# An input transposed by the loading DMA instead of TensorE, its first transform in 64-row tile pairs, and a rebuilt start order

## The chip, the core and the metric

The kernel runs on one core of a Trainium2 chip. The metric is the device time of one execution in microseconds. A core has five engines that run side by side, each through its own list of instructions in order: TensorE for matmuls (PE; its weight loads are shown apart as PEld), VectorE (DVE), ScalarE (ACT), GpSimd (POOL) and SyncE (SP). Engines wait for each other through semaphores. DMA transfers are issued from the queues of SP, ACT and POOL and all share 16 DMA engines. [...]

## What is computed

One input x (2048 rows of 640, bf16) goes through two branches, mixed row by row with a gate g.

```python
g = _sigmoid((x * gate_w).sum(-1, keepdims=True))
a = _A_ref(x, A_wqkv, A_wo)
b = _B_ref(x, B_A_re, B_A_im, B_B_re, B_B_im, B_C_re, B_C_im, B_log_dt, B_Dskip)
return g * a + (1 - g) * b
```

Branch A is attention with 32 heads of 20: q, k and v are projections of x, every position looks at 8 positions with distance 2, and the result is projected with wo. Branch B is a state-space convolution: for each of the 640 channels a filter K of 2048 taps is built from 192 complex modes (a sum of exponentials), and x is convolved with it through Fourier transforms of length 4096; x * Dskip is added.

## The kernel before

Everything is cut into tasks, 1,274 in the list `main` and 304 in `tail`. A task is added with `pl.add(name, engines, duration, function, ...)`. The order in which tasks are issued is not found at build time: `ORDER` is a table of numbers, one for each task, that gives the next task's index as a step from the last, with a letter where ACT or DVE may do it (A or D). `emit` walks the table and ties each engine's instructions together in that order.

The stages that the change and the prediction touch are these.

- **Loads of x and weights** (`Attn.loads`). `xl` holds four loads of x, 512 rows each; `wl` holds three loads of the projection weights (q, k, v) into the buffer `bufA`. They are issued on SP, between the parameter loads of `SSMParams.build` (`cre`, `bre`, `cim`, `bim`, `aim`, `are`, and the small `ldt`).
- **Turning x** (`Attn.window`). x arrives with positions on the partitions (tile `xn`). The projections need the 640 features on the partitions, so ten tasks `turn` multiply 128x128 blocks with an identity on PE, eight to a task, into the PSUM ring `ar`, and ten evictions `tev` put the result into `xT`, a part of `bufA`. The ring `ar` has two buffers (pool `pa`) and also serves the filter generator and the first transforms.
- **Projections** (`plan_late`, line 311, 300 matmuls of 512 columns, tile `tb`), evicted to `qA`, `kA`, `prj`, `pv` or `vst`. Each of the 60 evictions may be done by ACT or DVE.
- **The gate** (`plan_gate`, line 219): 80 narrow matmuls over all of `xT`.
- **Filter parameters** (`SSMParams.build`): a chain of operations on [128, 960] tiles over DVE and ACT, with logarithm, exponential and arctangent. Its ten results `pc` (a ring of four) are stored by SP to the DRAM tensor `Sprm` and read back as the tile `L`, by SP and, for one half of the first `L`, by POOL.
- **Filter generator** (`KGen.plan`): ten rounds. PE makes arguments from `L` (line 801), ACT takes sines (line 816) and exponentials (line 818) of them, DVE multiplies these (`pt`, `qq`), PE sums (line 856, `kps`), and ACT or DVE evicts to `E`.
- **Attention core** (`plan_core`): products on DVE (`prod`, line 375; `pv`, line 449), sums on PE, and the gated output `ga` (lines 489 and 491), all mixed with the generator's rounds.
- **First transforms** (`first`, line 1300): `f1` and `fk` for the filter, `fu` for the input (tile `Usb`). One `fu` task multiplies four 128x128 pieces with the 128x256 matrix `F1c`, which is block diagonal: rows of group g only meet columns of group g. `F1c` is block diagonal in four groups of 32 rows and 64 columns.
- **Tail** (`fft_conv`): the second transform (`fp`, line 1073), products of spectra, the inverse transforms (lines 1134 and 1164), the mix with the gate and the output. Its four PSUM buffers of `fp` are opened when all PSUM pools of `main` are closed.

## Time and profile before

| what | value |
|---|---|
| time of the runs, median (lowest, highest) of 3 | 336.16 us (335.34, 339.4) |
| span of the profiled execution | 335.4 us |
| granted TensorE clock, mean | 0.980 |
| DMA mean rate | 136 GB/s |
| x loads on SP | 4 of 640 KB |
| weight loads on SP | 3 of 800 KB |
| parameter loads on SP and ACT | 6 of 240 KB |
| turning matmuls on PE | 80, 264 ns each |
| first transform of the input on PE | 80, 275 ns each |

The profile comes from one execution. Its span (from the first to the last instruction) is 335.4 us; no time of that execution is given apart from its span, which stands 0.06 us above the fastest run and 0.8 below the median. Busy time of an engine is the time in which one of its instructions runs; matmuls overlap, so the mean of a matmul's length is longer than the time it adds. In rows of the timeline the first number is the start, the second the length; the bracket tells how long the engine had been idle and what ended that. In the page's second part the span is cut into 40 slices of 8.4 us, and a digit is the busy share in tenths.

### The profile page before, as it was taken

The numbers are of one execution on the slowest core, as the hardware profiler recorded it, in microseconds if no ns is written. First come the engines' busy times: TensorE is split into PE (matmuls) and PEld (weight loads), VectorE is DVE, ScalarE is ACT, GpSimd is POOL, SyncE is SP. The second block draws the span as 40 slices with busy tenths as digits, with TensorE's granted clock in tenths as the row PEclk, the third lists the DMA queues.
The fourth block names the chain that finished last, engine by engine and source line by source line (L and its number), as shares of the span: only waits on it lengthen the run. The fifth ranks groups of instructions, "written<-read, shape, count | busy, mean of one in ns | idle before, by whom it ended". The sixth has DMA issues, their size and how long they took to land. (4 is left out here: it accounts for less than half of the span.)

```text
span 335.4 us, 11982 instructions
## 1 busy us (share of the span) xinstructions
PE 285.5 (85%) x5181; PEld 171.0 (51%) x5214; DVE 294.2 (88%) x401; ACT 293.4 (87%) x433; POOL 62.3 (19%) x94
## 2 busy tenths in 40 slices
PE   0367999997899999999998799999999899996850
PEld 0334563444445555445554344556677676665740
DVE  1997988798989999999999979999686799999881
ACT  1789736999899999999999799999987889998990
POOL 8700043020005000101412341211040000000062
PEclk9999999999999999999999989999999999999985
DMA  8984435437107110524874887365565527666056
GB/s 253 356 264 113 119 91 159 86 91 170 26 9 153 27 24 8 149 62 141 199 190 119 186 208 161 93 118 124 154 207 221 180 64 216 159 123 100 4 136 182
DMA packets 45975, 45.68 MB, mean 136 GB/s; under 512 B 25098, under 2 KB 39738, under 8 KB 45922
## 3 DMA queue, kind: packets, MB, share of 16 engines
q1 hardware_dynamic: 39928, 27.90, 30.3%
q0 software_dynamic: 5248, 16.39, 20.2%
q8 instruction: 41, 0.67, 0.9%
q10 hardware_dynamic: 746, 0.61, 0.6%
q14 instruction: 12, 0.10, 0.1%
HBM read 30.88 MB, written 14.01 MB: 134 GB/s over the span
## 5 line engine op out<-in xcount | busy, mean ns | idle before, releaser
L311 PE MATMUL tb<-bufA 128*128 128x512 bf16 x267 | 73.5, 391 | 4.2 <-issue 1.4
L816 ACT ACTIVATE big<-ar 128x740 bf16<-128x740 int16 (+1 forms) x72 | 56.7, 858 | 1.4 <-PE ar L801 1.2
L818 ACT ACTIVATE big<-ar 128x848 bf16<-128x848 f32 x60 | 50.1, 905 | 0.2
L801 PE MATMUL ar<-Rarg,L 64*128 64x212 bf16 (+4 forms) x600 | 46.5, 253 | 3.5 <-ACT big L816 1.9
L449 DVE TENSOR_TENSOR pv<-vc,asb 128x2048 bf16<-128x2048 bf16 x40 | 48.2, 1217 | 0.3 <-PE tb L456 0.3
L311 PEld LDWEIGHTS <-bufA 128*128 128x128 bf16 x300 | 31.2, 122 | 28.5 <-issue 12.3
L856 PEld LDWEIGHTS <-pt 128*32 128x32 bf16 (+1 forms) x2560 | 25.3, 92 | 35.7 <-issue 33.2
L856 PE MATMUL kps<-qq,pt 128*32 128x21 bf16 (+1 forms) x2560 | 36.6, 173 | 6.0 <-issue 5.1
L838 DVE TENSOR_TENSOR pt<-big 128x1024 bf16<-128x1024 bf16 x48 | 32.8, 701 | 4.3 <-ACT big L816 2.2
L801 PEld LDWEIGHTS <-L 64*128 64x128 bf16 x600 | 20.8, 94 | 25.2 <-issue 22.4
L480 PE MATMUL tb<-wo_sb,oT 128*128 128x320 bf16 x160 | 29.9, 306 | 0.2
L507 ACT ACTIVATE sp_u<-fp 128x640 bf16<-128x640 f32 x31 | 23.9, 953 | 0.8 <-PE fp L1073 0.8
L375 DVE TENSOR_TENSOR prod<-prj 128x2048 bf16<-128x2048 bf16 x20 | 24.0, 1218 | 0.2 <-PE lg L381 0.2
L375 DVE TENSOR_TENSOR prod<-qA,kA 128x2048 bf16<-128x2048 bf16 x20 | 23.9, 1217 | 0.2 <-PE lg L381 0.2
L507 ACT ACTIVATE sp_k<-fp 128x640 bf16<-128x640 f32 x29 | 22.6, 969 | 1.1 <-PE fp L1073 1.1
L456 PE MATMUL tb<-pv,ind 128*64 128x512 bf16 (+1 forms) x192 | 23.2, 353 | 0.0
L368 POOL DMA_DIRECT2D vc<-vS x16 | 11.5, 723 | 59.0 <-DVE pv L449 55.0
L840 DVE TENSOR_TENSOR qq<-big 128x1344 bf16<-128x1344 bf16 x24 | 21.2, 883 | 0.0
L1191 POOL DMA_DIRECT2D out_dram<-ot x14 | 7.7, 558 | 72.3 <-DVE ot L1173 72.3
L1073 PEld LDWEIGHTS <-PHI 128*128 128x128 bf16 x160 | 15.5, 97 | 8.1 <-issue 1.1
L489 ACT ACTIVATE ga<-tb,g_sb 128x320 bf16<-128x320 f32 x29 | 15.6, 550 | 3.4 <-PE tb L480 3.1
L480 PEld LDWEIGHTS <-oT 128*128 128x128 bf16 x160 | 13.1, 98 | 7.1 <-issue 3.1
(171 smaller groups left out, 547.9 us busy)
## 6 DMA issues: line engine op xcount, KB each, us to landing
vc<-vS POOLq DMA_DIRECT2D x16, 327.5 KB, 6.4
xn<-in_A_x_dram SPq DMA_DIRECT2D x4, 640.0 KB
gaS<-ga SPq DMA_DIRECT2D x8, 320.0 KB
Usb<-in_A_x_dram POOLq DMA_DIRECT2D x8, 320.0 KB, 5.7
gaF<-gaS SPq DMA_DIRECT2D x8, 320.0 KB
bufA<-in_A_wqkv_dram SPq DMA_DIRECT2D x3, 800.0 KB
Sprm<-pc SPq DMA_DIRECT2D x10, 240.0 KB
L<-Sprm SPq DMA_DIRECT2D x76, 30.0 KB
```

Of the source, the lines that this page charges most:

```text
L311: nc.tensor.matmul(ppf, self.wq[:, which, kt, e::5], self.xT[:, c0 // 1024, kt, c0 % 1024:c0 % 1024 + SC], start=(kt == 0), stop=(kt == NK ...
L375: nc.vector.tensor_tensor(b[e][:], q[:, e, o:o + C].unsqueeze(1).to_broadcast([128, W, C]), win(k[:, e, :], o, W, DIL, C), ALU.mult)
L449: nc.vector.tensor_tensor(o, vw, b["asb"][:].unsqueeze(2).to_broadcast(sh), ALU.mult)
L456: nc.tensor.matmul(b["op", e][64 * a:64 * a + 64, 0:n, :], ind[:, 32:96], b["pv", e][:, w, a, 0:n, :], start=(w == 0), stop=(w == 3), skip ...
L480: nc.tensor.matmul(apf[:, :320], b["oT"][:, e, i * 128:(i + 1) * 128], wo_sb[:, e, hf * 320:(hf + 1) * 320], start=(e == 0), stop=(e == 4))
L507: nc.scalar.activation(o, i, ACT.Identity)
L801: nc.tensor.matmul(ar[:, g2, a0:a0 + ncol], L[rows, sb, gv, l0:l0 + 128], R[rows, c0:c0 + ncol], start=True, stop=True, tile_position=(64 ...
L816: nc.scalar.activation(d_[:, :, s0 * QW:s1 * QW], ar[:].bitcast(I16)[:, :, 0:2 * (s1 - s0) * QW:2], ACT.Sin, scale=SCL)
L818: nc.scalar.activation(dst[:, gp::2].rearrange("p g s n -> p g (s n)"), ar[:, :, 0:2 * EW], ACT.Exp)
L838: nc.vector.tensor_tensor(pt[:, :, k, :], gg[:, :, ::-1] if k else gg, e1, ALU.mult)
L840: nc.vector.tensor_tensor(qq[:], trg[:, :, KI:].rearrange("p a (v m) -> p a v m", v=2), exq[:, :, KI:].unsqueeze(2).to_broadcast([128, 32, ...
L856: nc.tensor.matmul(kps[32 * g:32 * g + 32, h, NM * ql:NM * ql + NM], pt[rows, k, v, :], qq[rows, k, v, :], start=(g not in started), stop= ...
```

## The change

The loads of x become DMA transposes that write `xT` directly. The tile `xn`, the ten turning tasks and their evictions are gone.

```diff
-        xr = self.x.rearrange("(i p) d -> p i d", p=128)
-        xl = [lambda sc=sc: nc.sync.dma_start(xn[:, 4 * sc:4 * sc + 4], xr[:, 4 * sc:4 * sc + 4]) for sc in range(4)]
+        xl = [lambda sc=sc: nc.sync.dma_start_transpose(self.xT[:, sc // 2, :, 512 * (sc % 2):512 * (sc % 2) + 512], self.x[512 * sc:512 * sc + 512]) for sc in range(4)]
...
-            def turn(_, hf=hf, kt=kt, b=b):
-                tx = b["tx"] = pa.tile([128, 2, 512], F32, name="ar")
-                for i in range(8):
-                    nc.tensor.matmul(tx[:, i // 4, (i % 4) * 128:(i % 4) * 128 + 128], self.xn[:, 8 * hf + i, kt * 128:(kt + 1) * 128], self.ident[:], start=True, stop=True)
-
-            def ev(en, hf=hf, kt=kt, b=b):
-                evict(nc, en, self.xT[:, hf, kt, :], b["tx"][:].rearrange("p a b -> p (a b)"))
```

The loads come in another order: log_dt first, x and weights in turn, the identity and the gate weights after the first exponential.

```diff
+        nc.scalar.dma_start(ldt[:], log_dt.rearrange("(p k) -> p k", k=5))
         load(nc.sync, "cre", C_re); load(nc.scalar, "bre", B_re)
         load(nc.sync, "cim", C_im); load(nc.scalar, "bim", B_im)
-        nc.scalar.dma_start(ldt[:], log_dt.rearrange("(p k) -> p k", k=5))
-        nc.scalar.dma_start(g5[:], gate_w.rearrange("(k p) -> k p", p=128))
-        at_.load_ident()
-        xl[0]()
         load(nc.sync, "aim", A_im)
-        xl[1]()
-        for w_ in wl:
-            w_()
+        xl[0](); wl[0](); xl[1](); wl[1]()
         load(nc.sync, "are", A_re)
-        xl[2](); xl[3]()
+        wl[2](); xl[2](); xl[3]()
...
         nc.scalar.activation(dtb[:], ldt[:], ACT.Exp)
+        nc.scalar.dma_start(g5[:], gate_w.rearrange("(k p) -> k p", p=128))
+        at_.load_ident()
```

Products with dt may now be made by ACT in five pieces, the sine table is loaded by a small operation of its own, and half of the first `L` is read by ACT's queue, not POOL's.

```diff
-            tt("tau", "tau", "aim", "dtc", ALU.mult, rdy=9.6)
+            scaled("tau", "aim", dtc, 9.6)
...
+        def scaled(o, a, m, rdy):
+            def fn(e):
+                if e == "D":
+                    V.tensor_tensor(t[o][:], t[a][:], m[:].unsqueeze(2).to_broadcast(SH), ALU.mult)
+                else:
+                    for k in range(5):
+                        SCA.activation(t[o][:, k], t[a][:, k], ACT.Identity, scale=m[:, k:k + 1])
...
+        self.warm = pl.add("wsin", "A", 0.2, lambda _: SCA.activation(sn[:], bias[0.5], ACT.Sin), after=[x for x in pl.tasks if "A" in x.dur], table="sin")
...
-                    (self.nc.gpsimd if gs == (1,) else self.nc.sync).dma_start(L[64 * g + 2:64 * g + 2 + 4 * NPC, :, v, l0:l0 + NST], src)
+                    (self.nc.scalar if gs == (1,) else self.nc.sync).dma_start(L[64 * g + 2:64 * g + 2 + 4 * NPC, :, v, l0:l0 + NST], src)
```

One `fu` task is now eight matmuls of 128 columns: rows 0 to 63 with the first half of `F1c`, rows 64 to 127 with the second. Its eviction reads the same 1024 values in another arrangement.

```diff
+                if name == "fu":
+                    by = b["by"] = b["bp"][:].rearrange("p a (b f) -> p (a b) f", f=64).rearrange("p (g q) f -> p g q f", g=4)
+                    for ql in range(4):
+                        for r in range(2):
+                            nc.tensor.matmul(by[:, 2 * r:2 * r + 2, ql], sf[64 * r:64 * r + 64, 4 * n + ql::st], P["F1c"][64 * r:64 * r + 64, 128 * r:128 * r + 128],
+                                             start=True, stop=True, skip_group_check=True, tile_position=(64 * r, 0))
+                    return
```

In the tail the first half of each `fp` pair takes its buffer from the ring `ar` of the main part, which stays open, and the second half from a new pool of two.

```diff
-                    fp = spec[nm, ro, h] = q["ps"].tile([128, 2, 512], F32, name="fp")
+                    fp = spec[nm, ro, h] = (q["ps"] if h else pa).tile([128, 2, 512], F32, name="fp", tag="fp" if h else "ar")
```

Both tables of `ORDER` are new throughout; of `main` the first numbers are shown.

```diff
 ORDER = {"main": (
-    "7 -7 15 -14 1 1166 -1164 56 -57 3 2 -3 6 1 1 39 -43 1 51A -8A -25 -14 2 38 1D 1 1A -32 33 1A -42 1 69 1 -57 72 -56 57 "
...
+    "1148 -1134 -14 52 1 2 -54 3 6 -8 1 3 1 1 3 1 -7 8 -4 18 -5 8 -15 1 7 8 -10 35 -2 3 10 1 1D 13 -3 -47D 48 -63 1 63D -47 "
```

What the new order does is shown at three places. First SP's queue at the start (`DMA` rows are loads and stores, `Sprm<-pc` the parameter results), before and then now:

```order
L583 DMA cre<-in_B_C_re_dram 128x960
L583 DMA cim<-in_B_C_im_dram 128x960
L186 DMA xn<-in_A_x_dram 128x4x640
L583 DMA aim<-in_B_A_im_dram 128x960
L186 DMA xn<-in_A_x_dram 128x4x640
L187 DMA bufA<-in_A_wqkv_dram 128x5x640 x3
L583 DMA are<-in_B_A_re_dram 128x960
L186 DMA xn<-in_A_x_dram 128x4x640 x2
L654 DMA Sprm<-pc 640x1x192 x10
```

```order
L561 DMA cre<-in_B_C_re_dram 128x960
L561 DMA cim<-in_B_C_im_dram 128x960
L561 DMA aim<-in_B_A_im_dram 128x960
L178 DMA_TRANSPOSE bufA<-in_A_x_dram 128x5x512
L179 DMA bufA<-in_A_wqkv_dram 128x5x640
L178 DMA_TRANSPOSE bufA<-in_A_x_dram 128x5x512
L179 DMA bufA<-in_A_wqkv_dram 128x5x640
L561 DMA are<-in_B_A_re_dram 128x960
L179 DMA bufA<-in_A_wqkv_dram 128x5x640
L178 DMA_TRANSPOSE bufA<-in_A_x_dram 128x5x512 x2
L639 DMA Sprm<-pc 640x1x192 x10
```

The first x and the first weights moved together to the front, the last two pieces of x to the end, and all four transposes still stand ahead of the parameter stores.

Second, ACT just ahead of the filter generator's first sine (`big<-ar 128x2x444`; `ge` and `om` belong to the gate, `qA`, `kA`, `prj`, `pv`, `vst` are evictions of projections, `sn` is the small sine), before and now:

```order
L507 ACTIVATE kA<-tb 128x512 x2
L507 ACTIVATE prj<-tb 128x512
L223 ACT_TABLE_LOAD
L223 ACTIVATE ge<-ar 128x16
L507 ACTIVATE pv<-tb 128x512
L239 ACTIVATE om_587<-ar 16x128
L816 ACT_TABLE_LOAD
L816 ACTIVATE big<-ar 128x2x444
```

```order
L485 ACTIVATE kA<-tb 128x512
L709 ACT_TABLE_LOAD
L709 ACTIVATE sn<-bc_159 128x1
L217 ACTIVATE om_463<-ar 16x128
L485 ACTIVATE prj<-tb 128x512
L752 DMA L_162<-Sprm 40x2x192 x4
L485 ACTIVATE pv<-tb 128x512
L485 ACTIVATE vst<-tb 128x512
L802 ACTIVATE big<-ar 128x2x444
```

The sine table moved five places ahead of the first sine, and four loads of `L` stand between the evictions.

Third, DVE at the end of the parameter chain (the operations on `at`, `t_144` or `t_146`, `pc`), before and now:

```order
L661 TENSOR_TENSOR pc<-at,t_144 128x960
L661 TENSOR_TENSOR pc<-t_144,t_143 128x960
L509 CAST bufA<-ar 128x1024 x3
L509 CAST kA<-tb 128x512
L375 TENSOR_TENSOR prod<-qA,kA 128x2048 x2
```

```order
L646 TENSOR_TENSOR pc<-at,t_146 128x960
L630 TENSOR_SCALAR t_145<-at 128x960
L646 TENSOR_TENSOR pc<-t_146,t_145 128x960
L205 TENSOR_SCALAR ge<-ge 128x16
L206 RECIPROCAL g_sb<-ge 128x16
L208 TENSOR_SCALAR omg<-g_sb 128x16
L210 CAST ob<-omg 128x16
L487 CAST prj<-tb 128x512
L353 TENSOR_TENSOR prod<-qA,kA 128x2048 x2
```

Three evictions of the turning that followed the last parameter are gone, and the gate's small operations stand there.

## The prediction

> **What bounds the kernel now.** I read the page's engine shares first, then the slices, then the busy time in two stretches (columns: stretch, length, busy time and instructions of PE, PEld, DVE, ACT, POOL, then clock, DMA share, GB/s), cut where the first sine of the filter generator starts.

> ```profile
> PE 285.5 (85%) x5181; PEld 171.0 (51%) x5214; DVE 294.2 (88%) x401; ACT 293.4 (87%) x433; POOL 62.3 (19%) x94
> ...
> ACT  1789736999899999999999799999987889998990
> ...
> 0.00:55.18 55.18, 36.24 (x283) 21.20 (x287) 43.94 (x53) 34.87 (x44) 17.72 (x26) 1.00 0.62 194
> 55.18:335.40 280.22, 249.28 (x4899) 149.84 (x4927) 250.24 (x348) 258.57 (x390) 44.62 (x69) 0.98 0.50 125
> ```

> ACT and DVE are level at 87 and 88%. From 55.18 us on ACT idles 280.22 - 258.57 = 21.65 us and DVE 29.98 us: a busy pair that hands work to and fro. Before 55.18 ACT idles 20.3 us, and its sixth slice (42 to 50 us) shows a 3. So there are two prices: work taken from the pair counts about half for each engine, and a microsecond off the start of the sines counts nearly in full. The timeline says what the sines wait for:

> ```profile
> 6.67 0.21 ACT L603 ACTIVATE dtb<-ldt 128x5 bf16<-128x5 bf16 x1 [2.19 <-DMA ldt<-in_B_log_dt_dram]
> 6.92 1.00 DVE L678 TENSOR_SCALAR dtc<-dtb 128x5 f32<-128x5 bf16 x1 [5.94 <-ACT dtb L603]
> 11.01 1.30 PEld L204 LDWEIGHTS <-xn 128*128 128x128 bf16 x13 [2.31 <-DMA xn<-in_A_x_dram]
> 21.55 3.95 PE L311 MATMUL tb<-bufA 128*128 128x512 bf16 x9
> 23.18 0.62 DVE L658 TENSOR_SCALAR pc<-tau 128x960 bf16<-128x960 f32 x1
> 23.83 1.16 DVE L661 TENSOR_TENSOR pc<-x,pc 128x960 bf16<-128x960 f32 x1
> 24.90 1.15 DVE L699 SCALAR_TENSOR_TENSOR xl<-xl,lnd 128x960 f32<-128x960 f32 x1
> 39.62 1.15 DVE L661 TENSOR_TENSOR pc<-t,t 128x960 bf16<-128x960 f32 x1
> 43.49 4.59 SPq L766 DMA_DIRECT2D L<-Sprm  x12
> 44.09 2.64 POOL L766 DMA_DIRECT2D L<-Sprm  x4 [29.57 <-DMA L<-Sprm]
> 44.69 2.14 PE L219 MATMUL ar<-gw_sb,bufA 128*128 128x1 bf16 x80
> 46.69 2.33 PE L311 MATMUL tb<-bufA 128*128 128x512 bf16 x9
> 48.95 0.61 PE L381 MATMUL lg<-prod,ind 128*32 128x512 bf16 x8
> 53.44 0.52 PE L801 MATMUL ar<-Rarg,L 64*128 64x296 bf16 x8
> 53.88 1.28 ACT L816 ACT_TABLE_LOAD   x1 [2.87 <-PE ar L801]
> ...
> L<-Sprm POOLq DMA_DIRECT2D x4, 30.0 KB, 2.7
> ```

> Two chains end there. The parameters finish on DVE at 40.8, and their round through DRAM fills L by about 49.4 (POOL's fourth issue ends at 46.73, plus a landing of 2.7, as the row of the DMA issues below says). PE reaches the first argument matmul (L801) only at 53.4, since its first projection (L311) had to wait until 21.55 for x to be turned and evicted. PE is the later chain; ACT then still loads the sine table.

> **The change, part by part.** All counts are from the two instruction orders; durations are from these groups (columns: line, engine, operation, tiles, shapes, count, then busy time, mean ns, idle before).

> ```profile
> L204 PE MATMUL ar<-ident,xn 128*128 128x128 bf16 x80 | 8.1, 264 | 8.4 <-ACT bufA L507 6.4 <-DMA xn<-in_A_x_dram 2.0
> L507 ACT ACTIVATE bufA<-ar 128x1024 bf16<-128x1024 f32 x6 | 6.0, 1018 | 1.1 <-PE ar L204 1.1
> L509 DVE CAST bufA<-ar 128x1024 bf16<-128x1024 f32 x4 | 4.7, 1215 | 0.0
> L489 ACT ACTIVATE ga<-tb,g_sb 128x320 bf16<-128x320 f32 x29 | 15.6, 550 | 3.4 <-PE tb L480 3.1
> L491 DVE TENSOR_SCALAR ga<-tb,g_sb 128x320 bf16<-128x320 f32 x3 | 1.6, 546 | 1.0 <-ACT big L507 1.0
> L507 ACT ACTIVATE E<-kps 128x336 bf16<-128x336 f32 x10 | 4.7, 471 | 1.3 <-PE kps L856 1.3
> L507 ACT ACTIVATE prj<-tb 128x512 bf16<-128x512 f32 x15 | 9.3, 636 | 1.4 <-PE tb L311 1.4
> L509 DVE CAST prj<-tb 128x512 bf16<-128x512 f32 x10 | 6.8, 688 | 5.8 <-PE tb L311 5.8
> ```

> *Work removed and shifted.* The 80 turning matmuls go (8.1 us of PE), and their ten evictions (6.0 us of ACT, 4.7 of DVE). Seven gate evictions (ga) move from ACT to DVE (3.8 us), three filter evictions (E, about 0.5 each) too, three prj evictions the other way (2.1 off DVE, 1.9 onto ACT). The product tau leaves DVE (1.15) and becomes five pieces on ACT, each near 0.35 (an estimate from 0.21 for 128x5 and 0.47 for 128x336), 1.75 together; dtc (1.0) leaves DVE. The single changes left cancel within 1 us. Sums: ACT -6.0 - 3.85 - 1.4 + 1.9 + 1.75 and small parts, about -7.3; DVE -4.7 + 3.8 + 1.5 - 2.1 - 1.15 - 1.0, with small parts about -4.0.

> *The parameters.* Log_dt is now loaded first and the first DVE product no longer stands behind dtc. The wait of SP's fourth load shows when bre had landed:

> ```profile
> 4.55 0.34 SPq L583 DMA_DIRECT2D aim<-in_B_A_im_dram  x1
> ...
> SPq L583 <- DMA bre<-in_B_B_re_dram: 2.4, 1, 2.4
> SPq L766 <- DMA Sprm<-pc: 1.9, 1, 1.9
> ...
> DVE t L624 <- ACT t L696: 2.0, 1, 2.0
> ```

> That was 4.5; with one small load ahead, DVE starts near 5.0 instead of 6.9. Up to the last piece DVE has 22 full products (1.07 from start to start, 23.83 to 24.90), 8 halves (0.6) and 2 casts (0.6): 23.5 + 4.8 + 1.3 = 29.6. Its wait for ACT's logs and exponentials was 2.0 us, with 0.3 after the arctangent; the chain is the same, so I keep 2.3: 5.0 + 29.6 + 2.3 = 37.0, against 40.8. From there to the first issue of L took 2.7 us (40.8 to 43.49, 1.9 of it landing). Four issues on SP and four on ACT side by side take 1.5 (12 took 4.59), landing about 2.3: L is full at 43.5.

> The four issues on ACT are a new wait in its queue: behind them stand the evictions of pv and vst, and PE needs the buffers these free for its last ten projections ahead of the sines. ACT passes at 37.0 + 2.7 + 1.5 = 41.2, evicts, PE follows by 43.5: no later than L itself. ACT gives up 1.5 us there in which it has nothing else. POOL's issues (2.64) disappear under idle time. The sine table is loaded earlier (wsin, 0.2), in a gap, so its 1.28 leaves the path.

> *PE's side.* When the first weights are in, 2,640 KB have come (five parameter tensors of 240, a quarter of x, 800 of weights); now 2,480 KB had come when the second xn landed, at 11.01. At 354 GB/s (the row below) the difference takes 0.5: about 12. Then 100 projections at 0.233 (the row at 46.69: ten, nine of them recorded, in 2.33), the gate 2.1, two logit groups 1.2, and 3 us of eviction waits as now: 12 + 23.3 + 2.1 + 1.2 + 3 = 41.6. L is the later one, so the first sine starts at about 44, 11 us sooner.

> *The transposing load* as such is not in the trace. Below: it moves like the plain one, at the 354 GB/s of the stretch from 10 to 20 us, hidden under the parameter work. Above: small packets.

> ```profile
> 10.00:20.00 10.00, 3.39 (x28) 3.00 (x29) 9.89 (x12) 8.37 (x10) 4.47 (x8) 1.00 1.07 354
> 20.00:30.00 10.00, 7.76 (x36) 3.97 (x37) 7.96 (x11) 8.82 (x10) 0.00 (x0) 1.00 0.51 154
> ...
> q1 hardware_dynamic: 39928, 27.90, 30.3%
> xn<-in_A_x_dram SPq DMA_DIRECT2D x4, 640.0 KB
> L423 SPq DMA_DIRECT2D aS<-at x32: 555/607/1475, 65.6 to 231.7; - x32
> ```

> This queue's packets took 0.303 x 16 x 335.4 / 39928 = 41 ns of an engine each, at 700 bytes. If x came in 256-byte pieces (128 columns of a row), 10,240 packets x 41 / 16 = 26 us instead of 7.4, so all loads would end near 44 rather than 25. SP's issue is bounded by the aS row: 607 ns for 256 rows, so up to 6 us for 2,560 pieces. I take the copy's rate, because the bytes and the target's 128 partitions are the same, and keep 44 for the range. [...]

> *The first transform* (fu, 80 matmuls of 256 columns becoming 160 in 64-row pairs) stands in a stage that PE bounds: 23.85 of 25 us busy, while DVE idles 5.7.

> ```profile
> 237.00:262.00 25.00, 23.85 (x190) 17.78 (x189) 19.30 (x29) 21.92 (x32) 4.37 (x8) 1.00 0.59 204
> 237.99 1.04 PE L1300 MATMUL bp<-F1c,Usb 128*128 128x256 bf16 x8
> 305.38 2.42 PE L1134 MATMUL cp<-GAB,Y 64*128 64x128 bf16 x80 [2.42 <-DVE Y L1104]
> ```

> Eight now take 1.04, so a group of four 0.52. Pairs of the same tile and width run at 2.42 / 80 = 30 ns in the tail: 0.24 for eight. PE saves up to 20 x 0.28 = 5.6 us, and I count 2 on the path, since ACT is at 21.9 of 25 there. The upper cost is a full matmul's length (264 ns in the L204 row) lost at each change of tile shape, twice in 20 groups: 10.6 us, a net loss of 5. [...] The tail now starts in a ring of the main part, and I count nothing for it.

> *The sum*, against the profiled execution, 335.4 us (the fastest run is 335.34, the median 0.8 above the span). Before the first sine ACT does 34.9 now; in the new order the six turning evictions (6.0) and two full operations (2.1) go, tau's pieces, three small ones and two more evictions come (1.75 + 0.6 + 1.2): 30.4. DVE does 43.9; four turning evictions, tau and dtc (6.85), one prod (1.2) and two casts (1.4) go, two half operations (1.25) come: 35.7. What is left is 293.4 - 7.3 - 30.4 = 255.7 and 294.2 - 4.0 - 35.7 = 254.5. With ACT's idle time of now: 44 + 255.7 + 21.7 = 321. With DVE's: 44 + 254.5 + 30.0 = 328.5, less 2 from the transform, 326.5. Since the change shifts evictions onto DVE I go near its end: a span of 325, a median of **325.5 us**.

> **The rivals.**

> *Transposing loads are slow* (the other side). The gate needs the last x piece, and 55 projections stand behind it on PE. At 44 us for the last piece: 44 + 2.1 + 12.8 + 1.2 = 60, first sine at 61, then 255.7 + 21.7 or 254.5 + 30.0: 338 to 345.5, **342**. It turns slower than before once the last x lands after 38, some 5 us for each load instead of 1.9. For it: the pieces are small and SP would issue for long. Against: the DMA share falls from 1.07 to 0.5 after 20 us, which leaves room. [...]

> *The earlier start is given back in the middle.* DVE bounds alone (328.5) and PE loses 2 to 4 us by changes of tile and by waits for rings in the new order: **331**. For it: DVE already waits 5.8 us for projections (the prj row). Against: PE, ACT and DVE all have less to do.

> *The removal does nothing beyond its work*: if the sines start at 55 as now because L or PE still come late, only half of 11.3 us is left, **330**.

> **How the numbers follow.** Forecast 0.62, slow loads 0.16 (0.02 of it for blocks with no overlap at all), given back 0.18, work alone 0.04. The forecast spans 319 to 329; with the rivals up to 339, range **317 to 339**. A change of 2% is about what a measurement of this kernel can tell from none: under 329.4, 0.70 (the forecast, a third of the middle rival and part of the last); over 342.9, 0.11 (the bad part of slow loads and reordering that costs more); within, 0.19.

> **What would show it.** Right: first projection on PE at 12 to 13 us, last pc near 37, first sine near 44, ACT busy 286 us and DVE 290, fu groups of eight in 0.25. Wrong: PE waiting for bufA's loads past 25 us, Sprm stores late because SP still issues transposes, or the last sine or exponential of the generator not at least 6 us earlier while DVE idles more than before.

## The result: 4.2% slower

The changed kernel takes 350.57 us in the median of its runs (350.24 to 351.07), the kernel before 336.24 beside it: a ratio of 1.0417, with a 95% interval of 1.0367 to 1.0467. Run once more beside other kernels it gave 353.94 (ratio 1.0455, interval 1.0399 to 1.0511). Forecast was 325.5, range 317 to 339. Here and below a median is taken over all runs of a kernel, while a ratio leaves out, on both sides, runs more than 1.5% above the kernel's fastest.

From the page of after (engine shares, granted clock by slices, the queues of SP and of PE's instructions):

```profile
PE 285.4 (82%) x5191; PEld 166.7 (48%) x5214; DVE 291.0 (83%) x401; ACT 288.6 (83%) x429; POOL 58.0 (17%) x90
...
PEclk9997699999999999988999958999699999999995
...
q1 hardware_dynamic: 48184, 27.90, 31.1%
...
q8 instruction: 40, 0.66, 0.7%
```

The work is what was forecast: ACT 288.6 us (286), DVE 291.0 (290). All of the loss is idle time. The clock row of before,

```profile
PEclk9999999999999999999999989999999999999985
```

has one 8 under full load; that of after has dips at 30 to 45, 140 to 170, 200 to 215 and 245 to 255 us. To place the loss, I cut both spans at the first sine, the end of the last sine and the first `fp` matmul (columns: stretch, length, busy time of PE, PEld, DVE, ACT, POOL, clock, DMA share, GB/s). Before, then after:

```profile
55.20:225.30 170.10, 158.37 (x3553) 82.58 (x3583) 158.25 (x215) 164.94 (x243) 31.09 (x45) 0.99 0.48 113
225.30:266.60 41.30, 38.91 (x516) 28.57 (x515) 34.47 (x49) 37.10 (x53) 5.82 (x10) 1.00 0.56 177
266.60:335.40 68.80, 51.98 (x832) 38.69 (x832) 57.52 (x86) 56.52 (x94) 7.70 (x14) 0.93 0.50 122
```

```profile
53.10:239.10 186.00, 167.72 (x3649) 89.74 (x3669) 163.37 (x222) 169.25 (x248) 26.04 (x40) 0.95 0.43 104
239.10:280.60 41.50, 33.20 (x508) 23.19 (x509) 31.01 (x45) 31.41 (x42) 3.95 (x6) 0.92 0.46 132
280.60:349.30 68.70, 52.00 (x834) 38.59 (x832) 58.32 (x88) 57.21 (x95) 7.70 (x14) 0.95 0.56 142
```

The sines start 2.1 us earlier instead of 11. The stage of the sines is 15.9 us longer: 4.3 are ACT work that the new order takes forward (169.25 against 164.94, and 5.7 less behind the last sine), 11.6 are ACT idle (16.75 against 5.16). From the last sine to the first `fp` it takes as long as before although PE, DVE and ACT have 3.5 to 5.7 us less to do there. The tail is the same.

### The start

SP's queue and DVE in after; then PE, whose matmuls of one projection (five) take 1.17 us at full clock, and two stretches with the clock and the DMA share (third and second column from the right):

```profile
2.18 5.68 SPq L178 DMA_TRANSPOSE bufA<-in_A_x_dram  x1
...
8.53 4.70 SPq L178 DMA_TRANSPOSE bufA<-in_A_x_dram  x1
...
14.94 11.22 SPq L178 DMA_TRANSPOSE bufA<-in_A_x_dram  x2
26.28 19.59 SPq L639 DMA_DIRECT2D Sprm<-pc  x10
48.05 5.61 SPq L752 DMA_DIRECT2D L<-Sprm  x12
```

```profile
31.63 1.16 DVE L646 TENSOR_TENSOR pc<-x,pc 128x960 bf16<-128x960 f32 x1 [4.56 <-DMA Sprm<-pc]
...
44.18 1.16 DVE L646 TENSOR_TENSOR pc<-t,t 128x960 bf16<-128x960 f32 x1
```

```profile
31.58 2.29 PE L289 MATMUL tb<-bufA 128*128 128x512 bf16 x5 [3.77 <-ACT qA L485]
```

```profile
20.00:30.00 10.00, 6.78 (x30) 3.33 (x29) 7.07 (x10) 5.86 (x7) 1.71 (x4) 1.00 1.09 248
30.00:40.00 10.00, 8.20 (x94) 4.40 (x95) 5.78 (x6) 6.81 (x9) 0.00 (x0) 0.57 0.81 185
```

Each transposing load holds SP for 4.7 to 5.7 us. The first `pc` is ready at 18.1, and its store is issued at 26.28, after all four. The ring of four `pc` tiles is full, DVE and ACT wait (7.1 and 4.1 us), ACT then evicts `qA` late (moves a projection's result out of `tb`), PE stands still for 3.77 us, and its next projection takes 2.29 us instead of 1.17: the clock granted from 31.4 to 41.7 us was 0.50, so 0.57 in the stretch of the row. The last `pc` ends at 45.3 (forecast 37.0; before 40.8), and `L` is asked for at 48.05.

### Where PE stops in the stage of the sines

The timeline of PE in after, all its idle times over 1 us between 60 and 250 us that no engine and no transfer ends (`issue` in the bracket):

```profile
110.72 0.19 PE L842 MATMUL kps<-qq,pt 128*32 128x21 bf16 x3 [1.71 <-issue]
...
146.63 0.27 PE L842 MATMUL kps<-qq,pt 128*32 128x21 bf16 x15 [2.03 <-issue]
...
159.45 0.42 PE L842 MATMUL kps<-qq,pt 64*32 64x21 bf16 x36 [1.06 <-issue]
...
182.58 0.56 PE L842 MATMUL kps<-qq,pt 64*32 64x21 bf16 x53 [2.46 <-issue]
...
206.42 0.55 PE L787 MATMUL ar<-Rarg,L 64*128 64x296 bf16 x4 [1.83 <-issue]
...
245.56 0.22 PE L842 MATMUL kps<-qq,pt 128*32 128x21 bf16 x6 [2.31 <-issue]
```

These are 11.4 us. Before had two such gaps:

```profile
84.30 0.26 PE L856 MATMUL kps<-qq,pt 128*32 128x21 bf16 x13 [1.92 <-issue]
...
191.39 0.27 PE L856 MATMUL kps<-qq,pt 128*32 128x21 bf16 x15 [2.36 <-issue]
```

```
kernel  block  starts   used up in  fetched  gap
before  2491   107.8    3.84        1.8      -
before  5819   184.5    4.36        5.5      2.5
before  6331   198.5    3.18        1.3      -
after   2491   107.5    1.36        2.0      1.9
after   4027   143.2    1.18        2.0      2.2
after   5307   176.3    3.63        4.7      2.6
after   6331   202.9    1.52        2.2      2.0
```

Landing is not enough: in after no block between 60 and 300 us starts sooner than 1.28 us after its packet has landed, and each gap in the table ends 1.3 to 1.5 us after it. So a gap is "fetched" plus some 1.4, less "used up in"; what passes in these 1.4 us the trace doesn't show.

A `kps` matmul with its weight load takes about 11 ns (2,560 have PE busy for 29.0 us). In the order before, 116 runs of `kps` have 32 or 64 instructions (one has 96), with other PE work between; in the new one there are 49, up to 384 long. So three blocks are used up in 1.2 to 1.5 us, where before none took under 3.1, and the next block isn't there. The other three gaps stand behind blocks that lasted 2.9 to 3.6 us and during which the fetch began only 2.4 to 3.3 us after the block's start. From 0.8 to 1.7 us after three of the six gaps (those that end at 146.6, 159.5 and 245.6), and after 200.7, where PE had waited 1.78 us for ACT, the clock records show a granted clock of 0.50 (half clock from here on), for 3.4, 3.4, 6.8 and 10.2 us: 23.9 us between 60 and 300, against 3.4 before.

### After the last sine

POOL and DVE in after:

```profile
238.41 0.57 POOL L978 DMA_DIRECT2D PHI<-c_phi  x1 [17.18 <-PE ar L787]
238.98 2.87 POOL L346 DMA_DIRECT2D vc<-vS  x4
...
247.91 5.77 DVE L427 TENSOR_TENSOR pv<-vc,asb 128x2048 bf16<-128x2048 bf16 x5 [4.96 <-DMA vc<-vS]
...
258.11 1.67 DVE L889 COPY X<-E 128x640 bf16<-128x640 bf16 x8 [3.31 <-PE bp L1293]
```

In the new order the third `PHI` load, which waits for the last argument matmul, stands ahead of two pairs of `vc` loads in POOL's queue. DVE waits 4.96 us for `vc`, and the expansion `X`, behind those products in DVE's list, starts 19.0 us after the last sine (11.5 before). The filter's last transforms hang on `X`.

### The profile page after: what moved, and what is told of

Its sections match the earlier page's. It is cut to its first block, busy times and chain, and to the rows that moved or that the text cites. A ratio compares the mean times of both kernels' runs of the same rounds, so it can differ in the third digit from the quotient of the medians.

```text
span 349.3 us, 11953 instructions
## 1 busy us (share of the span) xinstructions
PE 285.4 (82%) x5191; PEld 166.7 (48%) x5214; DVE 291.0 (83%) x401; ACT 288.6 (83%) x429; POOL 58.0 (17%) x90
## 3 DMA queue, kind: packets, MB, share of 16 engines
q1 hardware_dynamic: 48184, 27.90, 31.1%
## 5 line engine op out<-in xcount | busy, mean ns | idle before, releaser
L289 PE MATMUL tb<-bufA 128*128 128x512 bf16 x277 | 79.3, 415 | 12.6 <-ACT qA L485 6.1
L427 DVE TENSOR_TENSOR pv<-vc,asb 128x2048 bf16<-128x2048 bf16 x40 | 47.2, 1219 | 12.0 <-PE tb L434 6.9
L289 PEld LDWEIGHTS <-bufA 128*128 128x128 bf16 x300 | 32.4, 124 | 46.1 <-issue 20.7
L787 PE MATMUL ar<-Rarg,L 64*128 64x212 bf16 (+4 forms) x600 | 47.7, 258 | 5.3 <-issue 1.8
L842 PE MATMUL kps<-qq,pt 128*32 128x21 bf16 (+1 forms) x2560 | 29.0, 176 | 10.9 <-issue 10.1
L842 PEld LDWEIGHTS <-pt 128*32 128x32 bf16 (+1 forms) x2560 | 24.1, 92 | 21.7 <-issue 20.0
L824 DVE TENSOR_TENSOR pt<-big 128x1024 bf16<-128x1024 bf16 x48 | 32.1, 702 | 2.7 <-ACT big L802 1.5
L458 PE MATMUL tb<-wo_sb,oT 128*128 128x320 bf16 x160 | 27.6, 305 | 4.8 <-DVE oT L487 2.2
L485 ACT ACTIVATE big<-bp 128x1024 bf16<-128x1024 f32 x16 | 16.1, 1029 | 9.6 <-PE bp L1289 9.6
L485 ACT ACTIVATE sp_u<-fp 128x640 bf16<-128x640 f32 x30 | 21.5, 918 | 0.7 <-PE fp L1058 0.7
L485 ACT ACTIVATE sp_k<-fp 128x640 bf16<-128x640 f32 x30 | 21.5, 924 | 0.6 <-PE fp L1058 0.6
L458 PEld LDWEIGHTS <-oT 128*128 128x128 bf16 x160 | 14.1, 99 | 13.5 <-issue 5.3
L346 POOL DMA_DIRECT2D vc<-vS x16 | 11.5, 736 | 33.3 <-DVE pv L427 29.0
```

The source lines that it names most:

```text
L289: nc.tensor.matmul(ppf, self.wq[:, which, kt, e::5], self.xT[:, c0 // 1024, kt, c0 % 1024:c0 % 1024 + SC], start=(kt == 0), stop=(kt == NK ...
L427: nc.vector.tensor_tensor(o, vw, b["asb"][:].unsqueeze(2).to_broadcast(sh), ALU.mult)
L458: nc.tensor.matmul(apf[:, :320], b["oT"][:, e, i * 128:(i + 1) * 128], wo_sb[:, e, hf * 320:(hf + 1) * 320], start=(e == 0), stop=(e == 4))
L485: nc.scalar.activation(o, i, ACT.Identity)
L787: nc.tensor.matmul(ar[:, g2, a0:a0 + ncol], L[rows, sb, gv, l0:l0 + 128], R[rows, c0:c0 + ncol], start=True, stop=True, tile_position=(64 ...
L824: nc.vector.tensor_tensor(pt[:, :, k, :], gg[:, :, ::-1] if k else gg, e1, ALU.mult)
```

## The experiments

The first theories: (A) the transposing loads hold SP's queue and so the parameters; (B) PE runs out of instructions; (C) the new order's waits cost the time; (D) `vc` behind `PHI`.

**Plain loads of x** (`e1_plain_x`).

```diff
-nc.sync.dma_start_transpose(self.xT[...], self.x[512 * sc:512 * sc + 512])
+nc.sync.dma_start(self.xT[...], self.x[512 * sc:512 * sc + 512].rearrange("(p i) d -> p (i d)", i=4)...)
```

> The changed kernel with x loaded by plain copies of the same bytes into the same places, so that x is not transposed and the values are other ones. Theory A (the transposing loads hold SP's queue for 4.7 to 5.7 us each, the Sprm stores stand behind them and the ring of four pc tiles runs full): the x issues take under 2 us each, no pc waits (7.1 us on DVE now), last pc near 38 instead of 45.3, first sine near 45 instead of 53.05, time 341 to 344. Rival (the bytes on the DMA engines are late, whatever their form): first projections and pc waits stay, first sine after 50, 347 to 351. Neither expects the stage between the first and the last sine (185.9 us now) to get shorter by more than 2 us.

348.84 us, ratio to before 1.0188 (1.0064 to 1.0312). SP's queue, and the sines (minimum, median and maximum length in ns, then first and last start):

```profile
9.35 5.53 SPq L178 DMA_DIRECT2D bufA<-in_A_x_dram  x2
17.85 22.72 SPq L639 DMA_DIRECT2D Sprm<-pc  x10
```

```profile
L802 ACT ACTIVATE big<-ar x72: 771/808/958, 47.7 to 227.0; 128x740 bf16<-128x740 int16 x48, 128x888 bf16<-128x888 int16 x24
```

The first store goes out at 17.85, no `pc` waits, the last one ends at 40.0, and the sines start 5.4 us earlier than with transposes. The transposing costs that much at the start, less than the 8 expected. The stage of the sines stays long: 182.6, where a change of up to 2 us from 186 was expected. The ratio is 2.3% under that of the changed kernel, some 8 us.

**Stores by POOL** (`e2_store_pool`).

```diff
-op(f"sp{i}", "S", 0.36, lambda _: nc.sync.dma_start(Sv[:, :, i, :], t[k][:]), ...)
+op(f"sp{i}", "G", 0.36, lambda _: nc.gpsimd.dma_start(Sv[:, :, i, :], t[k][:]), ...)
```

> The changed kernel with the ten Sprm stores issued by POOL instead of SP; the transposing loads stay. Theory A (SP's queue): the pc waits of DVE (7.1 us) go, last pc at 38 to 40, first sine at 46 to 48 unless PE's cold projections (31.6 to 41.7 us) become the later chain, then 50; time 344 to 347. Rival (the landing of the transposes on the DMA engines is what is late): Sprm lands late all the same, first sine stays at 53, 350.

357.06 us, 1.0596 (1.0513 to 1.068); the first sine comes at 54.6. POOL and DVE:

```profile
18.19 0.83 POOL L639 DMA_DIRECT2D Sprm<-pc  x1 [3.64 <-DVE pc L643]
...
33.69 1.16 DVE L646 TENSOR_TENSOR pc<-x,pc 128x960 bf16<-128x960 f32 x1 [5.76 <-DMA Sprm<-pc]
```

The store is issued 8 us earlier, and DVE still waits 5.76 us for a store to land. SP's queue, as theory A had it, is not all that counts: the stores land late whoever issues them, among and behind the transposes' packets (the first store's packets moved from 23.0 to 26.3, the last of the transposes' at 32.8). POOL's stores went in larger packets, mostly of 4,224 bytes instead of 384, so the run changes more than the queue. In the records of the changed kernel the 10,240 pieces of 256 bytes took 21.1 ns each, 13.5 us of all 16 engines; in those of `e1_plain_x` the plain ones of 1,024 bytes took 8.1 us.

**Seven tiles in the ring** (`e6_ring7`).

```diff
-pcs = ctx.enter_context(tc.tile_pool(name="sp_pc", bufs=4, side="right"))
+pcs = ctx.enter_context(tc.tile_pool(name="sp_pc", bufs=7, side="right"))
```

> The changed kernel with seven pc tiles in the ring instead of four. If the full ring is what holds the parameters (pc waits of 4.56, 2.52 and 4.12 us), the waits go and the last pc ends at 39 instead of 45.3; L then at 42, first sine at 46 to 48, time 343 to 346. Rival (the stores themselves are late, behind 10,240 packets of the transposes, and PE's projections are cold and late): the last pc ends early but the first sine stays above 51, time 349 to 351.

The last `pc` ends at 38.5 and the first sine is at 47.0, 6.1 earlier, as the first theory said. But the time is 352.0 (1.0388, 1.0312 to 1.0464): the stage of the sines is 190.8 us, with 41 us at half clock. Here the earlier start was lost again while PE stopped later on; with plain loads, where it was nearly as early, it was not, so that an earlier start alone decides nothing.

**The block boundaries moved** (`e3_shift69`, `e4_shift49`).

```diff
         nc.scalar.activation(at_.gw[:], lt[:, 0, 0:5], ACT.Identity)
+        for _ in range(69):
+            nc.tensor.matmul(lt[:, 1, 0:5], g5[:], at_.ident[0:5, 0:5], start=True, stop=True)
```

> The changed kernel with 69 matmuls of 5 columns added at the head of PE's list, at a time when PE waits for its first loads: 138 instructions, so that every later boundary of a 256-instruction block falls 138 instructions earlier in the work. Theory B (PE runs out of instructions where a long run of short kps matmuls uses up a block before the next one has been fetched, and its clock is then halved): the idle time of PE put down to issue in the stretch 100 to 250 us falls from 11.4 to 3 to 6 us, half-clock intervals there from 23.9 to under 10 us, time 340 to 346. Rival C (the new order's waits on DMA and other engines cost the time, the gaps of PE are their sign): no change, 349 to 352.

> The same with 49 matmuls, 98 instructions: by the times of the runs in the trace this puts the boundaries where the long kps runs use up most of a block. Theory B: issue gaps of PE 12 to 17 us in all, time 350 to 356, at least 6 above the kernel with 69. Rival C: no change, 349 to 352, and no difference between the two.

345.0 us (1.0129, 1.0032 to 1.0226) and 349.0 (1.0331, 1.0244 to 1.0419). With 69 the stage of the sines falls to 177.7 and the gaps over 1 us there to one; with 49 it falls to 179.9, where it should have grown. Half-clock time is 17.1 and 23.9 us, more than theory B gave. For B in the one, against its numbers in the other; undecided.

**PHI behind vc** (`e5_phi_last`), an edit of the list that the table gives:

```diff
+            p = next(t for t in out if t.name == "phi2")
+            n = max(out.index(t) for t in out if t.name.startswith("vc"))
+            if out.index(p) < n:
+                out.remove(p)
+                out.insert(n, p)
```

> The changed kernel with one load moved in POOL's queue: the third PHI load, which waits for the last argument matmul (17.2 us at 238.4), goes behind the last two pairs of vc loads instead of ahead of them. Theory D (the vc loads stand behind PHI and hold DVE): DVE's wait of 4.96 us for vc at 242.9 to 247.9 goes, X starts 12 to 14 us after the last sine instead of 19.0, the time from the last sine to the first fp matmul falls from 41.5 to 35 to 37 us, whole time 344 to 347. Rival (PE's gap of 2.3 us at 243 and the half clock of 6.8 us behind it set that stage): 40 us or more remain, 349 to 351.

353.05 us, runs from 343.64 to 358.47: too wide a spread for a ratio, so only the stage is read. POOL's `vc` loads are issued before the wait, and `X` starts 14.7 us after the last sine:

```profile
231.68 1.47 POOL L352 DMA_DIRECT2D vc<-vS  x2
235.80 1.42 POOL L352 DMA_DIRECT2D vc<-vS  x2 [2.65 <-DVE pv L433]
249.04 0.57 POOL L984 DMA_DIRECT2D PHI<-c_phi  x1 [11.82 <-PE ar L793]
```

From the last sine to the first `fp` it takes 37.4 instead of 41.5. Of the kernels below with the same edit, `e8_all3` and `e14_kc_late` take 36.9 and 37.0; `e12_two` takes 40.0, against 43.3 in `e6_ring7`, which lacks only this edit. In `e12_two` the wait for `vc` is gone too, but DVE waits 6.6 us there for PE's results ahead of `X`, 4.0 in this run. Theory D holds for this stage, for 3.3 to 4.1 us.

**The first transform in full matmuls** (`e7_fu_full`).

```diff
-                        for r in range(2):
-                            nc.tensor.matmul(by[:, 2 * r:2 * r + 2, ql], sf[64 * r:64 * r + 64, ...], P["F1c"][64 * r:64 * r + 64, ...], ..., tile_position=(64 * r, 0))
+                        nc.tensor.matmul(b["bp"][:, ql, :], sf[:, 4 * n + ql::st], P["F1c"][:], start=True, stop=True)
```

> The changed kernel with the first transform (fu) in full 128-row matmuls of 256 columns, 80 instead of 160, as before. Theory: the pairs save 4.0 us of PE (a group takes 0.32 us instead of 0.52), in a stage that is not bound by PE (33.2 of 41.5 us busy): no change, 349 to 352. Rival 1 (the pairs' gain counts): 353 to 355. Rival 2 (changes of tile shape cost more than the pairs save): 345 to 348.

354.51 us (1.0481, 1.0409 to 1.0552), above the changed kernel's 350.57 and 353.94 by 4 and by less than 1 (ratios 1.0417 and 1.0455, their intervals overlap this one): whether the pairs' gain counts is not settled.

**Three edits together** (`e8_all3`): 69 small matmuls, `phi2` behind `vc`, seven tiles.

> Three of the edits together: 69 small matmuls at the head of PE's list, the PHI load behind the vc loads, seven pc tiles. If the three costs are what they seem (start 5 to 7 us, middle 8 us, the stage after the last sine 5 us) and add up, 330 to 336; if they hide each other or the new order costs the rest by itself, 338 to 345.

335.46 us, 0.9877 (0.9832 to 0.9922): level with the kernel before or slightly faster (1.2% by the ratio, 0.5% by the medians, 335.46 against 337.26), although the seven tiles alone had brought nothing.

**PE's list rearranged** (`e9_spread`). The core of the rule, applied after each 64 instructions of `kps` in a row; `mid` is what stands between. `e11_best` adds the seven tiles and `phi2` behind `vc`.

```diff
+                        if x.eng == "P" and not kmm(x) and not any(d in mid for d in x.deps + x.after) and ...:
+                            out.insert(i + 1, out.pop(j))
```

> The changed kernel with its list of PE work rearranged by a rule, the other engines' lists kept: after 64 instructions of kps matmuls in a row the next piece of other PE work whose inputs are there is taken ahead, so that 49 runs of up to 384 instructions become 81, of which 77 have 32 or 64. Theory B (PE outruns the loading of its own instructions in long kps runs, and the clock is halved after the gap): gaps of over 1.5 us at block boundaries all but vanish, half-clock time between 60 and 300 us falls from 23.9 to under 10 us, the stage between the first and the last sine from 186.0 to 174 to 178, time 338 to 343. Rival C (the new order's waits on other engines and DMA cost the time): that stage stays above 182, time 347 to 352.

> The changed kernel with the rearranged PE list, seven pc tiles and the PHI load behind the vc loads. If the three costs are right and independent: first sine near 47, the stage of the sines 174 to 178, 37 from the last sine to the first fp, 69 to the end, 327 to 331. If an earlier start is lost again in the middle, as with the seven tiles alone: 333 to 340.

358.82 (1.0654, 1.0548 to 1.076) and 347.1 us (1.0226, 1.0128 to 1.0323). Theory B's numbers fell: gaps of 0.9 to 4.4 us stay at the same boundaries, since the pieces between are short too; the blocks from 2491 and 4027 are now used up in 2.1 us instead of 1.4 and 1.2. It is not the length of the runs that counts but the time in which a whole block is used up. Why the first of the two is slower still isn't known.

**The reverse in the kernel before** (`e10_gather`). `kmm` tasks hold the `kps` matmuls, `t` is the fourth of its unit:

```diff
+            for t in [t for t in out if t.name.startswith("kmm") and t.name[-1] == "3"]:
+                for x in [x for x in out if x.name.startswith(t.name[:-1]) and x is not t]:
+                    out.remove(x)
+                    out.insert(out.index(t), x)
```

> The kernel before with the reverse edit: of each four kps pieces the first three are held back to stand directly ahead of the fourth on PE, so that 116 runs of 32 or 64 instructions become 30 of 128 or 256; nothing else is moved and x is loaded and turned as before. Theory B: gaps at block boundaries come up, 8 to 16 us in all, half-clock time rises from 3.4 to 15 to 35 us, time 343 to 352. Rival (PE's gaps follow from late data and other engines, or from the transposing loads): 335 to 339.

342.94 us (1.017, 1.0085 to 1.0256), but with idle times of 1.1 and 1.3 us only at the boundaries and no half clock between 60 and 300 us. So the time comes from elsewhere; DVE's wait for `kps` ahead of `pt` (6.8 us in the stage of the sines) fits the work held back, but no run separates it. It doesn't speak for B.

**The same three edits without the small matmuls, with a whole block of them, and with 200 instructions** (`e12_two` without the loop, `e15_block128` with `range(128)`, `e16_block100` with `range(100)`; `e13_again` is the changed kernel). These decide between B and the rest, since only the boundaries differ.

> The kernel with three edits less the 69 small matmuls: only seven pc tiles and the PHI load behind the vc loads. If the place of the block boundaries in PE's list is worth as much as the two kernels with and without them say, 343 to 350, at least 8 above the kernel with three edits (335.46); gaps at boundaries 11 to 15 us again, half-clock time over 20 us between 60 and 300. Rival: the two other edits brought the gain, 334 to 339.

> The changed kernel itself once more, beside the others on this chip: 349 to 352 by all theories.

> The kernel with three edits, with 128 small matmuls at the head of PE's list instead of 69: 256 instructions, one whole block, so that the boundaries fall where they fall with none. If it is the place of the boundaries that counts: 345 to 351, as with none (348.74), the gaps at the same work (kps runs at some 105, 141, 177 and 203 us). Rival (the small matmuls help by themselves, by a warm PE or a later start): 333 to 338.

> The same with 100 small matmuls, 200 instructions. From the times between instructions in the changed kernel's trace with the gaps taken out, blocks that PE uses up in under 3.5 us fall short by 3.4 us in all with 200, 2.9 with 138 and 7.3 with none. If that is the mechanism, 333 to 340, near the one with 138 and at least 7 under the one with 256. Rival as above: no difference among 138, 200 and 256.

| instructions added | 0 | 138 | 200 | 256 |
|---|---|---|---|---|
| median, us | 348.74 | 335.46 | 336.12 | 348.23 |
| lowest to highest, us | 344.82 to 352.26 | 330.89 to 342.89 | 330.52 to 370.47 | 344.31 to 350.13 |
| ratio to before | 1.0305 (1.025 to 1.036) | 0.9877 (0.9832 to 0.9922) | 0.9851 (0.9798 to 0.9903) | 1.029 (1.0237 to 1.0343) |

A whole block of added instructions changes nothing, part of one takes 12 to 13 us off by the medians (14 to 15 by the ratios), at two different places, both picked beforehand from the trace. The timelines of PE with none added, with 256, and with 138:

```profile
141.88 0.29 PE L848 MATMUL kps<-qq,pt 128*32 128x21 bf16 x15 [2.30 <-issue]
...
177.95 0.56 PE L848 MATMUL kps<-qq,pt 64*32 64x21 bf16 x53 [2.93 <-issue]
...
203.93 0.55 PE L793 MATMUL ar<-Rarg,L 64*128 64x296 bf16 x4 [2.51 <-issue]
```

```profile
140.77 0.29 PE L850 MATMUL kps<-qq,pt 128*32 128x21 bf16 x15 [2.30 <-issue]
...
177.13 0.56 PE L850 MATMUL kps<-qq,pt 64*32 64x21 bf16 x53 [3.21 <-issue]
...
204.84 0.55 PE L795 MATMUL ar<-Rarg,L 64*128 64x296 bf16 x4 [3.15 <-issue]
```

```profile
171.04 0.61 PE L365 MATMUL lg<-prod,ind 128*32 128x512 bf16 x6 [1.64 <-issue]
...
196.66 0.28 PE L850 MATMUL kps<-qq,pt 64*32 64x21 bf16 x17 [2.98 <-issue]
```

With none and with 256 the gaps stand at the same work, down to the count of matmuls behind each (15, 53, 4); with 256 there is one more, 2.79 at 200.0. With 138 there are two, elsewhere. The clock by slices says what hangs on it (none, then 138):

```profile
PEclk9999999999999999898989858999688999998995
```

```profile
PEclk9979999979999999999999879999979999997995
```

**The first kc load later** (`e14_kc_late`), on top of the three edits:

```diff
+            for x in [t for t in out if t.name in ("xld0S", "xld0G")]:
+                out.remove(x)
+                out.insert(next(n for n, t in enumerate(out) if t.name == "phi0" or t.name[:2] == "f1"), x)
```

> The kernel with three edits (335.46), and the first kc load (640 KB, first used some 25 us later) moved back: its SP half behind the next ga store, its POOL half one vc load on, out of the stretch in which kc, asb, L, ga, vc and Usb all move (DMA share 1.0 for 20 us from 178 on). Theory E (this jam holds the engines): ACT's wait of 4.73 us for the ga store and PE's of 2.85 us for L fall under 1.5 us each, 330 to 333. Rival (the jam moves on with it, or kc then comes too late for its transform): 334 to 338.

335.56 us, 0.9928 (0.9891 to 0.9965). Of the waits between 170 and 215 us with three edits,

```profile
ACT ga L473 <- DMA gaS<-ga: 4.7, 1, 4.7
...
PE ar L795 <- DMA L<-Sprm: 3.1, 2, 2.9
```

the first has fallen to 1.1 and the second is gone, and the time is the same: PE's gap ahead of 193 us is 3.62 instead of the 2.98 ahead of 196. The rival holds.

**The boundaries moved in the kernel before** (`e17_before74`): the loop of small matmuls above, `range(74)`, in the kernel before.

> The kernel before with 74 small matmuls at the head of PE's list, 148 instructions. In its trace no block of 256 instructions is used up in under 3.1 us between 60 and 310 us, so that wherever the boundaries fall the blocks last about as long as a fetch takes; of all places this is one of the worst, short by 1.8 us in all for a fetch of 3.5 us. Theory: the kernel before doesn't depend on the place of the boundaries, 336 to 339. Rival (moving the boundaries is worth 13 us in any kernel of this length): 330 or 345 and more.

335.18 us, 0.9943 (0.9903 to 0.9983). In its profile the gaps of before are gone but one of 0.96 us. The place is worth 0.6% here (at most 1.0% by the interval), 13 us in the new order.

## Why the prediction was wrong, point by point

- **First projection at 12 to 13, work on ACT and DVE 286 and 290**: right (12.99; 288.6 and 291.0). DVE's chain of 37.0 us was right but for the waits: with seven tiles it ended at 38.5.
- **The transposing load "moves like the plain one"**: wrong, and named in advance as a sign. The bound on SP's issue, "up to 6 us", was close (4.7 to 5.7) but stood outside the sum; the packets' number was right (10,240), their cost 13.5 us of all engines, between the 7.4 and the 26 of the bounds. What was missed is who stands behind: the `Sprm` stores, hence the ring of four, hence DVE, ACT and a PE at half clock. First sine 53.1 instead of 44: 9 us. Of these, 5.4 go with plain loads and 6.1 with seven tiles; the first sine then comes at 47.7 and 47.0, and no run says where the last 3 us lie.
- **"With ACT's idle time of now"**: this step failed most. It carried 21.7 us of idle time over to an order in which every engine's list is another one. Measured after the first sine: 296.25 - 257.91 = 38.3, with work of 257.9 against 255.7 forecast. 9 + 16.6 + 2.2 is the whole 28 between the lower sum, 321, and the span of 349.3. The sum by DVE, to which the forecast stands nearer, failed at the same step: 43.5 us idle instead of 30.0. In place of the old idle time the runs show PE stopping at block boundaries, the half clock that followed some of these stops, and `vc` behind `PHI`. With the three edits ACT's idle time falls from 38.3 to 32.1, and to 28.9 with the `kc` load later; what is still above 21.7, some 7 to 10 us, no run explains.
- **The rival "slow transposing loads"** had its price from x landing at 44; the last piece left at 27.7, and the rival's condition (after 38) was never met. The 0.02 for blocks with no overlap at all stands on nothing that a run shows: the 10,240 packets of the four loads, 21.1 ns each, all lay between 5.6 and 27.7 us, on average some ten of them under way at once. **"Given back in the middle"** named the right place, with 2 to 4 us of PE where ACT's idle time grew by 16.6, and another mechanism: tile changes and rings, not the fetching of instructions.
- **The pairs**: from the timeline of after,

```profile
261.47 0.54 PE L1289 MATMUL bp<-F1c,Usb 64*128 64x128 bf16 x8
...
263.18 0.86 PE L1289 MATMUL bp<-F1c,Usb 64*128 64x128 bf16 x16
```

  a second group directly behind the first adds 0.32 us, not 0.24. The 0.52 for four full ones was half of a row of eight, with the start of the row in it; a row of four in before,

```profile
245.07 0.60 PE L1300 MATMUL bp<-F1c,Usb 128*128 128x256 bf16 x4
```

  leaves 1.04 - 0.60 = 0.44 for the second group. Like for like a group saves 0.06 (alone, 0.60 to 0.54) to 0.12 us, 1.2 to 2.4 us of PE in 20 groups, not 5.6, and not the 4 that the expectation of `e7_fu_full` has. That the 2 us of the sum come off the path no run shows. A full matmul's length lost at each change of tile doesn't show either: a group alone is no longer than before.

Left open: why the fetch of some blocks begins only 2.4 to 5.3 us after the block ahead was started (in after from 135 us on; in before it began 3.5 to 4.1 us after at four blocks; transfers crowd there, but no run separated that), and what the half clock costs apart from the gap ahead of it.

## What to carry to other kernels

Idle time belongs to an order, not to a kernel: where a change rewrites the order of all engines, the old idle time may be a guess for the new one, but no term of a sum. Look at how short PE's instructions are as well as how long they take together: in this kernel PE stopped with nothing to wait for where 256 instructions went by in 1.2 to 1.5 us (in the table above some 2 us to the landing of the next block and 1.4 more), and some small matmuls at the head of the list were a cheap way to test it. A new load is priced by its issue time, its packets, and by whatever is queued behind it in the same ring.

## What was not expected of the hardware

A gap of 1.06 us was followed by 3.4 us at half clock. Between 60 and 300 us of after the half-clock times are 3.4, 6.8 or 10.2 us long, and the idle times ahead of them were 1.06 to 2.31 us. Other gaps of 1.71 and 2.46 us in the same trace were followed by none, so that the length of a gap alone doesn't tell. And 138 instructions that do nothing, in a list of some 10,430 (5,214 matmuls, each with its weight load), moved the time by 13 us.
